# Weight copies within DRAM in small pieces, each behind a one-element read, and a plan that counts the softmax in full

## The chip, the cores and the metric

The kernel runs on one core of one Trainium2 chip. The metric is device time in microseconds (us) for one execution; lower is better. Five engines work from queues of their own: TensorE (PE, matmuls, with PEld its weight loads), VectorE (DVE), ScalarE (ACT), GpSimd (POOL) and SyncE (SP, which here issues transfers only). An engine takes its instructions strictly in order; between engines there are semaphores. A transfer is issued by SP, POOL or ACT and carried out by 16 DMA engines that they share. Unless a text says "the median", times are those of one profiled execution.

## The reference

A layer normalisation feeds two branches whose results are added to the input: a windowed attention and a ReLU network of two layers. All is in float32.

```
x: 2048 x 576;  wqkv: 576 x 1728;  wo: 576 x 576;  w1: 576 x 4608;  w2: 4608 x 576
xn  = (x - mean) / sqrt(var + 1e-5)
qkv = xn @ wqkv                      # 32 heads of 18
logits[s, w] = q[s] . k[s - 2 w] * 18**-0.5,   w = 0..7, masked where s - 2 w < 0
attn = softmax over the 8 offsets;   o[s] = sum_w attn[s, w] v[s - 2 w]
out = x + o @ wo + relu(xn @ w1) @ w2
```

## The kernel before

**Tiles and stages.** The 2048 rows are taken in two phases of 1024 (even and odd rows); a dilation of 2 stays within a phase. A phase is 8 tiles of 128 rows, in two halves. The 4608 columns of w1 go in 18 sets of 256. One pass is one set for one half, so there are 18 x 2 passes in a phase and 72 in all (`g` = 0 to 71, set `m = g // 2`). In a pass TensorE makes h transposed, 128 columns of w1 by 256 rows at a time (four such blocks a pass), and then multiplies the h of the pass before by w2 into the PSUM banks `po`. Float32 products are built of rounded high and low parts: ACT writes the high part of a block (`hhi`, with the ReLU), DVE the low part (`hlo`), and three products are summed. From the third set on, a pass computes its four blocks in seven steps (P1, P5, P6, P2, P7, P3, P4) in a Strassen manner, for which DVE forms sums of parts of w1 (`ts`) and ACT and DVE split them into `wset`.

**Attention** is done for 8 heads at a time (a unit, four in a phase). In the passes of sets 0, 3, 7 and 11 of the first phase (1, 4, 8 and 12 of the second) TensorE makes q, k and v of the unit (`qkv_tile`, into `pm`), the halo rows of k and v are shifted by transfers, and then VectorE does the attention of the unit as background work: 8 products with k and 8 sums over 18 (`pr`, `lg`), the softmax (`sm_max`, `sm_sub` with an exponential on ACT, `sm_sum`, `sm_rcp`, `sm_div`), then products with v and adds, and a transpose. The result goes through DRAM (`turned`) and is multiplied by wo some passes later. POOL sets the mask (`affine_select`, line 862) and clears two rows ahead of each unit (`memset`, lines 793 and 794).

**The order of the work.** `Order` (lines 54 to 187) decides while the program is built in which order each engine gets its instructions. TensorE's order is written out by hand: `pe` gives its next group, and before it does, `step` gives out all ACT and DVE operations that the plan's own clocks would start by then, the one with the earliest due time first. The operations of the attention (`later`) wait in a list of their own (`back`) and go in, in order, where DVE would be free. So the plan's idea of how long a DVE or ACT operation takes, for DVE `n / 960.0 + 0.062` us with `n` elements per partition (line 143), settles which instructions stand ahead of which. In `attention` the softmax is entered as `add(sm_max, n, [z])`, then `sm_sub` with a lag of 0.8, `sm_sum` with `n`, `sm_rcp` with 64 and `sm_div` with `n`, where `n` is 512 (lines 940 to 944).

**Weight copies.** Each part of the weights is first copied within DRAM into a packed tile of its own: `W1C[n]` (576 x 256) and `W2C[n]` (256 x 576) for each set, `WQC[u]` for each unit, `WOC` (lines 399 to 417). POOL issues these copies, one transfer for each. Nothing holds a copy back but what stands ahead of it in POOL's queue. SP's loads of weights into SBUF read the packed tiles and wait for the copies (`set_make`, `w2_make`, `wq_make`, `wo_make`); SP's queue is in order too. Places in the passes are given by `at(g, idx, f, ...)`: `f` is called at tick `idx` of pass `g`, a tick being one group of matmuls. The copies of set 1 stand in the prologue, after the loads of x (lines 1123 and 1124); those of a later set `m` stand in pass `2 m - 3`.

Of the kernel before, what the change touches and what calls it, by code (L numbers as in the profile page):

```python
# [16 lines left out]
P = 128  # L17
# [10 lines left out]
QP = ((0, 3, 7, 11), (1, 4, 8, 12))  # L28
# [25 lines left out]
class Order:  # L54
# [92 lines left out]
    def later(self, fn, n, after=(), lag=0.0):  # L147
        op = Op(DVE, n / 960.0 + 0.062, fn, after, FAR, lag)
        self.back.append(op)
        return op  # L150

# [39 lines left out]
def tile_body(ctx: ExitStack, tc: tile.TileContext, x, wqkv, wo, w1, w2, out):  # L191
# [211 lines left out]
    O16 = dram.tile([P, NI, DR], F32, name="o16")  # L403
    kept = {}

    def w1_keep(n):
        kept["w1", n] = o_.keep(lambda: nc.gpsimd.dma_start(W1C[n], w1[:, 2 * n * P : 2 * (n + 1) * P]), 590)

    def w2_keep(n):
        kept["w2", n] = o_.keep(lambda: nc.gpsimd.dma_start(W2C[n], w2[2 * n * P : 2 * (n + 1) * P, :]), 590)  # L410

    def wq_keep(u):
        src = wqkv.rearrange("r (s c) -> r s c", s=3)[:, :, u * UD : (u + 1) * UD]
        kept["wq", u] = o_.keep(lambda: nc.gpsimd.dma_start(WQC[u], src), 1000)

    def wo_keep():
        kept["wo"] = o_.keep(lambda: nc.gpsimd.dma_start(WOC, wo), 1300)

    SETOK = {}
    ts_free = [[]]  # L420
# [7 lines left out]
    def set_early(m):  # L428

        src = W1C[m % NP][0:256, P : 2 * P].rearrange("(k p) c -> p k c", p=P)  # L430
        TSGOT[m] = send(lambda: nc.sync.dma_start(TS[:, 1], src), 128, [kept["w1", m % NP], *ts_free[0]])

    def set_make(m, plain=False, fine=False):

# [7 lines left out]
        def rest_rows():  # L442
            for rows in slice(0, DR), slice(DR, P):
                got[RR] = send(
                    lambda rows=rows: nc.sync.dma_start(z[rows, RR].rearrange("p k c -> p (k c)"), W1C[n][KT * P : D, :]),
                    64, [kept["w1", n], *free], late,
                )

        for rows, f, s in ((0, 0, B11), (0, 1, B12), (256, 1, B22), (256, 0, B21)):
            if s == B12 and m in TSGOT:  # L450
                got[s] = TSGOT.pop(m)
                rest_rows()
                continue
            ts = s == B12 and not plain
            dst = TS[:, 1] if ts else z[:, s]
            src = W1C[n][rows : rows + 256, f * P : (f + 1) * P].rearrange("(k p) c -> p k c", p=P)
            got[s] = send(
                lambda dst=dst, src=src: nc.sync.dma_start(dst, src), 128, [kept["w1", n], *free, *(ts_free[0] if ts else [])], late
            )
            if s == B12:  # L460
                rest_rows()
# [37 lines left out]

    def w2_make(m, f):  # L500
        W2[m, f] = w = w2p.tile([P, 2, D], F32R, name="w2t")
        g = send(lambda: nc.sync.dma_start(f32(w[:, 1]), W2C[m % NP][f * P : (f + 1) * P]), 295, [kept["w2", m % NP]], 4.0)
        W2OK[m, f] = hi_lo(w[:, 0], w[:, 1], f32(w[:, 1]), D, [g], 7 + 2 * f)

    WQOK = {}
# [1 line left out]
    def wq_make(p, u, kts, raw=None):  # L507

        w = wqset(p)
        b = (p + 1) % 2  # L510
        v = wqkv.rearrange("r (s c) -> r s c", s=3)[:, :, u * UD : (u + 1) * UD] if raw is not None else WQC[u]
        for kt in kts:
            z = raw[:, kt] if raw is not None else f32(w)[:, 1, kt]
            after = [] if raw is not None else [kept["wq", u]]
# [13 lines left out]
    def wo_make(ph, u):  # L528
        WO[ph, u] = w = vp.tile([P, 2, D], F32R, name="v")
        z = f32(w)[:, 1]  # L530
        got = []
        if u < NU:
            got.append(send(lambda: nc.sync.dma_start(z, WOC[u * UD : u * UD + P, :]), 295, [kept["wo"]], 3.0))
        else:
            for b in (0, DR):
                for v in range(NU):
                    got.append(send(
                        lambda b=b, v=v: nc.sync.dma_start(z[b + 16 * v : b + 16 * v + 16], WOC[v * UD + P : (v + 1) * UD, :]),
                        37, [kept["wo"]], 3.0,
                    ))  # L540
        WOOK[ph, u] = hi_lo(w[:, 0], w[:, 1], z, D, got, 8)

# [9 lines left out]
    def h_alloc(key):  # L552
        H[key] = hp.tile([P, TBN], F32R, name="hhi"), hp.tile([P, TBN], F32R, name="hlo")

    def h_parts(key, src, after, slack, alloc=True):

        def high():
            h_alloc(key)
            copy(H[key][0], src, AF.Relu)

        def low():
            hi, lo = H[key]
            nc.vector.scalar_tensor_tensor(lo, src, 0.0, f32(hi), op0=ALU.max, op1=ALU.subtract)  # L563
# [270 lines left out]
    def attention(ph, u, halo):  # L834
# [34 lines left out]

        def sm_sub():  # L870
            nc.vector.tensor_tensor(s["lg"], s["lg"], spread(s["m"]), op=ALU.subtract)
            nc.scalar.activation(s["lg"], s["lg"], AF.Exp, scale=scale)

        def sm_sum():
# [89 lines left out]
    for m in range(2, NPH * NP):  # L964
# [12 lines left out]
    at(14, 4, w1_keep, 0)  # L977
    at(14, 5, w2_keep, 0)
    for m in range(2, NPH * NP):
        for f in range(2):  # L980
            at(2 * m - 1, 2 * f, w2_make, m, f)
# [200 lines left out]
    set_make(1, True)  # L1182
    for f in range(2):
        w2_make(1, f)
    halo(0, 0)
    classic(1, 1, 0, "bk2")
    classic(1, 1, 1, "bkA")
# [68 lines left out]
```

## Time and profile before

| what | value |
|---|---|
| median of 3 runs | 1171.18 us (1170.12 to 1175.57) |
| profiled execution, its own time | 1173.04 us |
| its span | 1171.2 us |
| TensorE busy | 1135.0 us, 97% of the span |
| VectorE busy | 819.2 us, 70% |
| ScalarE busy | 754.1 us, 64% |
| GpSimd busy | 63.4 us, 5% |
| moved by DMA | 115.6 MB, 28.9 MB of it by POOL's queue |

A row of the groups of instructions has the source line, engine and operation, the tiles written and read, a count, the busy time, the mean duration of one and the idle time of the engine ahead of them. A row of the timeline has the start and the duration in us, and in brackets how long the engine had been idle and what ended that. A row of the waits has who waited for whom, the total in us, how often and the longest. A row of the transfers has the size of one and the median time from issue to landing. A row of the windows has the stretch, its length and TensorE's busy time in it, the granted clock, the share of the DMA engines and GB/s. In the profile w1's opening loads go into a tile named `v`, and those of the opening qkv weights into `kk`.

### The profile page before, as it was taken

What the parts mean: (1) busy time and instruction counts of PE and PEld (TensorE: products, weight loads), DVE (VectorE), ACT (ScalarE), POOL (GpSimd) and SP (SyncE); (2) the same over time, 40 slices, a digit from 0 to 9 for tenths busy, and PEclk for the clock granted to TensorE, in tenths of its full rate; (3) what the DMA queues carried; (4) which work ended last, traced back from release to release, by engine and by line L of the source; (5) the groups of instructions that cost most, each with busy time, mean ns of one, the idle gap of its engine ahead of it and who ended that gap; (6) DMA issues with size and microseconds to landing.
All of it is one profiled execution on the core that took longest, in us unless ns stands there. A gap on an engine that the chain in (4) does not pass through costs nothing.

```text
span 1171.2 us, 21895 instructions
## 1 busy us (share of the span) xinstructions
PE 1135.0 (97%) x8528; PEld 1115.0 (95%) x8528; DVE 819.2 (70%) x1533; ACT 754.1 (64%) x1658; POOL 63.4 (5%) x97
## 2 busy tenths in 40 slices
PE   7999999999998999999989999999999999999998
PEld 6899999999998999999989999999999999999998
DVE  6649979952998169964783299589926995399831
ACT  5558567755766477676685577477737765576764
POOL 2200201010011001000110000000000000000000
PEclk8999999999999999999999999999999999999999
DMA  6442532762245232433262222231323212321322
GB/s 202 156 121 67 167 97 73 243 188 73 74 145 181 45 97 71 133 83 115 90 192 66 71 70 64 41 106 49 96 45 90 70 53 63 93 62 57 74 76 91
DMA packets 133544, 115.60 MB, mean 99 GB/s; under 512 B 54128, under 2 KB 112240, under 8 KB 133120
## 3 DMA queue, kind: packets, MB, share of 16 engines
q1 hardware_dynamic: 128192, 85.00, 26.1%
q0 software_dynamic: 5104, 28.90, 7.7%
q8 instruction: 67, 1.10, 0.4%
q14 instruction: 37, 0.30, 0.1%
q10 hardware_dynamic: 144, 0.29, 0.1%
HBM read 96.01 MB, written 36.50 MB: 113 GB/s over the span
## 4 chain that ended last, share of the span: by engine, by line
PE 69%; DVE 19%; DMA 5%; ACT 4%; issue 3%; POOL 0%; SPq 0%; POOLq 0%; DVEq 0%; ACTq 0%
PE po L285 29%; PE bk L285 20%; PE pm L285 15%; PE bkA L285 4%; DVE pr L886 2%; DVE hlo L563 2%; DVE wset L282 2%; DVE pr L893 2%; DVE lg L859 2%; DMA olo<-turned 2%; DVE ts L282 1%; DVE pr L856 1%; DMA wset<-w1c 1%; ACT po L279 1%; DVE sn L282 1%
## 5 line engine op out<-in xcount | busy, mean ns | idle before, releaser
L285 PE MATMUL po<-w2t,hhi 128*128 128x256 f32 (+1 forms) x2304 | 397.2, 294 | 2.4 <-ACT po L279 2.4
L285 PEld LDWEIGHTS po<-w2t,hhi 128*128 128x128 f32 x2304 | 335.9, 188 | 4.5 <-ACT po L279 3.6
L279 ACT ACTIVATE x<-po 128x576 f32<-128x576 f32 x286 | 185.6, 649 | 147.5 <-PE po L285 144.0
L285 PE MATMUL po<-w2t,hlo 128*128 128x256 f32 (+1 forms) x1152 | 244.6, 293 | 0.7 <-DVE hlo L563 0.7
L285 PE MATMUL bk<-xs,wset 128*128 128x256 f32 x1632 | 234.4, 279 | 8.5 <-DVE hlo L563 8.5
L285 PEld LDWEIGHTS bk<-xs,wset 128*128 128x128 f32 x1632 | 212.0, 189 | 12.7 <-DVE hlo L563 12.2
L285 PEld LDWEIGHTS po<-w2t,hlo 128*128 128x128 f32 x1152 | 190.7, 188 | 0.9 <-DVE hlo L563 0.9
L279 ACT ACTIVATE po<-x 128x576 f32<-128x576 f32 x286 | 186.9, 654 | 6.2
L285 PE MATMUL pm<-wset,xa 128*128 128x432 f32 x768 | 171.8, 360 | 1.1 <-DVE wset L282 0.9
L285 PEld LDWEIGHTS pm<-wset,xa 128*128 128x128 f32 x768 | 140.5, 188 | 8.5 <-DVE wset L282 1.9
L285 PE MATMUL bk<-xa,wset 128*128 128x256 f32 x924 | 132.6, 281 | 7.0 <-ACT xa L279 4.0
L285 PEld LDWEIGHTS bk<-xa,wset 128*128 128x128 f32 x924 | 120.8, 191 | 8.4 <-ACT xa L279 4.3
L282 DVE TENSOR_TENSOR sn<-bk,sn 128x256 f32<-128x256 f32 x136 | 57.3, 421 | 97.7 <-PE bk L285 55.5
L279 ACT ACTIVATE kk<-pm 128x144 f32<-128x144 f32 (+1 forms) x68 | 21.1, 310 | 121.8 <-PE pm L285 120.0
L282 DVE TENSOR_TENSOR w2t<-w2t 128x576 fp32r<-128x576 f32 (+1 forms) x72 | 53.9, 748 | 64.2 <-ACT w2t L279 63.8
L279 ACT ACTIVATE hhi<-sn 128x256 fp32r<-128x256 f32 x136 | 56.1, 413 | 46.7 <-DVE sn L282 45.5
L886 DVE TENSOR_TENSOR pr<-lg,v 128x1152 f32<-128x1152 f32 x64 | 85.1, 1352 | 0.1
L856 DVE TENSOR_TENSOR pr<-qo,kk 128x1152 f32<-128x1152 f32 x64 | 84.6, 1350 | 0.0
L859 DVE TENSOR_REDUCE lg<-pr 128x64 f32<-128x1152 f32 x64 | 84.2, 1344 | 0.0
L285 PE MATMUL bk<-xr,wset 128*128 128x256 f32 x426 | 83.7, 278 | 0.0
L282 DVE TENSOR_TENSOR wset<-wset 128x512 fp32r<-128x512 f32 (+2 forms) x120 | 71.5, 600 | 12.7 <-ACT wset L279 12.4
L279 ACT ACTIVATE wset<-wset 128x512 fp32r<-128x512 f32 (+2 forms) x120 | 65.4, 550 | 10.4 <-DMA wset<-wqc 8.3
(132 smaller groups left out, 1355.2 us busy)
## 6 DMA issues: line engine op xcount, KB each, us to landing
w2t<-w2c SPq DMA_DIRECT2D x70, 288.0 KB, 3.0
wset<-w1c SPq DMA_DIRECT2D x106, 128.0 KB, 2.4
w1c<-in_w POOLq DMA_DIRECT2D x18, 576.0 KB, 7.9
w2c<-in_w POOLq DMA_DIRECT2D x18, 576.0 KB, 8.7
wset<-wqc SPq DMA_DIRECT2D x28, 216.0 KB, 2.7
out<-x SPq DMA_DIRECT2D x16, 288.0 KB, 2.2
wset<-w1c SPq DMA_DIRECT2D x70, 64.0 KB, 2.2
ts<-w1c SPq DMA_DIRECT2D x34, 128.0 KB, 2.6
```

The lines of the kernel that those rows point to most:

```text
L279: nc.scalar.activation(o, i, func)
L282: nc.vector.tensor_tensor(o, a, b, op=op)
L285: nc.tensor.matmul(o, l, r, start=start, stop=stop, skip_group_check=True)
L563: nc.vector.scalar_tensor_tensor(lo, src, 0.0, f32(hi), op0=ALU.max, op1=ALU.subtract)
L856: nc.vector.tensor_tensor(pr[i], q, window(k, i), op=ALU.mult)
L859: nc.vector.tensor_reduce(s["lg"][:, i], pr.pop(i).rearrange(heads, d=Dh), axis=AX.X, op=ALU.add)
L886: nc.vector.tensor_tensor(pr[i].rearrange(heads, d=Dh), e, window(v, i).rearrange(heads, d=Dh), op=ALU.mult)
L893: nc.vector.tensor_tensor(o, z[:, 0:n], z[:, n : 2 * n], op=ALU.add)
```

## The change

Three things change.

1. A copy within DRAM is cut into 4 pieces (w1 and w2 of a set), 6 (a unit's qkv weights) or 8 (wo). There were 41 copies and there are 176 pieces, of 147 to 166 KB. Ahead of each piece POOL copies one element of the `hhi` that was given out last (`LATEST`) into `spare`. Every piece has a place of its own: the pieces of w1 for set `m` at ticks 0, 2, 4 and 6 of pass `2 m - 3`, those of w2 at ticks 1, 3, 5 and 7 of pass `2 m - 2`, and so on.
2. The copies of set 1 move from the prologue's loads to behind the seventh tile's transposes, and those of w1 for set 2 into the prologue behind them.
3. The plan counts `sm_max` and `sm_sum` with `2 n`, `sm_rcp` with `n - 30`, and the exponential as an ACT operation of its own with no due time; every DVE operation gets 0.068 instead of 0.062 us, every ACT operation 0.07 instead of 0.06.

TensorE's instructions stay in their order. On SP, one unit's five transfers of the turned result move behind nine others; on ACT and DVE many operations trade places.

```diff
     def act(self, fn, n, after, slack, lag=0.0):
-        op = Op(ACT, n / 1120.0 + 0.06, fn, after, self.now() + slack, lag)
+        op = Op(ACT, n / 1120.0 + 0.07, fn, after, self.now() + slack, lag)
...
     def dve(self, fn, n, after, slack, lag=0.0):
-        op = Op(DVE, n / 960.0 + 0.062, fn, after, self.now() + slack, lag)
+        op = Op(DVE, n / 960.0 + 0.068, fn, after, self.now() + slack, lag)
...
-    def w1_keep(n):
-        kept["w1", n] = o_.keep(lambda: nc.gpsimd.dma_start(W1C[n], w1[:, 2 * n * P : 2 * (n + 1) * P]), 590)
-
-    def w2_keep(n):
-        kept["w2", n] = o_.keep(lambda: nc.gpsimd.dma_start(W2C[n], w2[2 * n * P : 2 * (n + 1) * P, :]), 590)
...
+    LATEST = []
+
+    def kept_part(key, dst, src, kb):
+
+        def f():
+            nc.gpsimd.tensor_copy(spare[0:1], f32(LATEST[-1])[0:1, 0:1])
+            nc.gpsimd.dma_start(dst, src)
+
+        kept.setdefault(key, []).append(o_.keep(f, kb))
+
+    def w1_keep(n, z):
+        rows = slice(144 * z, 144 * (z + 1))
+        kept_part(("w1", n), W1C[n][rows], w1[rows, 2 * n * P : 2 * (n + 1) * P], 147)
+
+    def w2_keep(n, z):
+        kept_part(("w2", n), W2C[n][64 * z : 64 * (z + 1)], w2[2 * n * P + 64 * z : 2 * n * P + 64 * (z + 1), :], 147)
...
             h_alloc(key)
+            LATEST.append(H[key][0])
             copy(H[key][0], src, AF.Relu)
...
             nc.vector.tensor_tensor(s["lg"], s["lg"], spread(s["m"]), op=ALU.subtract)
+
+        def sm_exp():
             nc.scalar.activation(s["lg"], s["lg"], AF.Exp, scale=scale)
...
-        a = add(sm_max, n, [z])
-        a = add(sm_sub, n, [a], 0.8)
-        a = add(sm_sum, n, [a])
-        add(sm_rcp, 64)
+        a = add(sm_max, 2 * n, [z])
+        a = add(sm_sub, n, [a])
+        a = act(sm_exp, n, [a], FAR)
+        a = add(sm_sum, 2 * n, [a])
+        add(sm_rcp, n - 30)
         add(sm_div, n)
...
         if m < NP:
-            at(max(2, g - 1), 0, w1_keep, m)
-            at(max(2, g - 1), 2, w2_keep, m)
+            for z in range(4):
+                if m > 2:
+                    at(g - 1, 2 * z, w1_keep, m, z)
+                at(g, z if m == 2 else 2 * z + 1, w2_keep, m, z)
     for u in range(NU):
-        at(2 * QP[0][u] - 3 if u else 12, 4, wq_keep, u)
-    at(8, 4, wo_keep)
...
+        for z in range(6):
+            at(2 * QP[0][u] - 3 + z // 3 if u else 13 + z // 3, 4 * (z % 3) + 3, wq_keep, u, z)
+    for z in range(8):
+        at(7 + z // 4, 3 * (z % 4) + 2, wo_keep, z)
...
         x_first(i)
-    w1_keep(1)
-    w2_keep(1)
...
     turn_one(7)
+    for z in range(4):
+        w1_keep(1, z)
+    for z in range(4):
+        w2_keep(1, z)
```

More of the change, by code (lines that the diff above doesn't have):

```diff
@@ L147, in later @@
     def later(self, fn, n, after=(), lag=0.0):
-        op = Op(DVE, n / 960.0 + 0.062, fn, after, FAR, lag)
+        op = Op(DVE, n / 960.0 + 0.068, fn, after, FAR, lag)
         self.back.append(op)
@@ L404, in tile_body, with wq_keep, wo_keep @@
     kept = {}
-    def w1_keep(n):
-        kept["w1", n] = o_.keep(lambda: nc.gpsimd.dma_start(W1C[n], w1[:, 2 * n * P : 2 * (n + 1) * P]), 590)
-    def w2_keep(n):
[L410 to L417, printed above, removed]
+    LATEST = []
[9 more added lines that the diff above has]
+        kept_part(("w2", n), W2C[n][64 * z : 64 * (z + 1)], w2[2 * n * P + 64 * z : 2 * n * P + 64 * (z + 1), :], 147)
+    def wq_keep(u, z):
+        rows = slice(96 * z, 96 * (z + 1))
+        src = wqkv.rearrange("r (s c) -> r s c", s=3)[rows, :, u * UD : (u + 1) * UD]
+        kept_part(("wq", u), WQC[u][rows], src, 166)
+    def wo_keep(z):
+        rows = slice(72 * z, 72 * (z + 1))
+        kept_part(("wo",), WOC[rows], wo[rows], 166)
     SETOK = {}
@@ L445, in rest_rows @@
                     lambda rows=rows: nc.sync.dma_start(z[rows, RR].rearrange("p k c -> p (k c)"), W1C[n][KT * P : D, :]),
-                    64, [kept["w1", n], *free], late,
+                    64, [*kept["w1", n], *free], late,
                 )
@@ L457, in set_make @@
             got[s] = send(
-                lambda dst=dst, src=src: nc.sync.dma_start(dst, src), 128, [kept["w1", n], *free, *(ts_free[0] if ts else [])], late
+                lambda dst=dst, src=src: nc.sync.dma_start(dst, src), 128, [*kept["w1", n], *free, *(ts_free[0] if ts else [])], late
             )
@@ L501, in w2_make @@
         W2[m, f] = w = w2p.tile([P, 2, D], F32R, name="w2t")
-        g = send(lambda: nc.sync.dma_start(f32(w[:, 1]), W2C[m % NP][f * P : (f + 1) * P]), 295, [kept["w2", m % NP]], 4.0)
+        g = send(lambda: nc.sync.dma_start(f32(w[:, 1]), W2C[m % NP][f * P : (f + 1) * P]), 295, kept["w2", m % NP], 4.0)
         W2OK[m, f] = hi_lo(w[:, 0], w[:, 1], f32(w[:, 1]), D, [g], 7 + 2 * f)
@@ L513, in wq_make @@
             z = raw[:, kt] if raw is not None else f32(w)[:, 1, kt]
-            after = [] if raw is not None else [kept["wq", u]]
+            after = [] if raw is not None else list(kept["wq", u])
             free = slots_free(b, range(432 * kt // 256, min(7, (432 * kt + 431) // 256) + 1))
@@ L532, in wo_make @@
         if u < NU:
[L533 removed]
+            got.append(send(lambda: nc.sync.dma_start(z, WOC[u * UD : u * UD + P, :]), 295, kept["wo",], 3.0))
         else:
@@ L538, in wo_make @@
                         lambda b=b, v=v: nc.sync.dma_start(z[b + 16 * v : b + 16 * v + 16], WOC[v * UD + P : (v + 1) * UD, :]),
-                        37, [kept["wo"]], 3.0,
+                        37, kept["wo",], 3.0,
                     ))
@@ L1175, in tile_body @@
     turn_one(7)
+    for z in range(4):
+        w1_keep(1, z)
+    for z in range(4):
+        w2_keep(1, z)
     s1 = s_forms(1, 32)
@@ L1184, in tile_body @@
         w2_make(1, f)
+    for z in range(4):
+        w1_keep(2, z)
     halo(0, 0)
```

6 lines of the change are left out of this document (3 added, 3 removed).

## The prediction

> **What bounds the kernel now.** I read the page first, then TensorE's busy time in stretches, then what TensorE waited for in those stretches.
>
> ```profile
> PE 1135.0 (97%) x8528; PEld 1115.0 (95%) x8528; DVE 819.2 (70%) x1533; ACT 754.1 (64%) x1658; POOL 63.4 (5%) x97
> ```
> ```profile
> 0.00:35.00 35.00, 25.24 (x136) 0.85 0.53 169
> ...
> 200.00:540.00 340.00, 332.82 (x2533) 0.99 0.42 121
> 540.00:620.00 80.00, 72.22 (x558) 0.98 0.47 142
> 620.00:1140.00 520.00, 515.70 (x3914) 1.00 0.25 68
> ```
>
> TensorE is the bound: 1135.0 of 1171.2 us busy. Its instructions and their order stay, so the change can win only from the idle rest, some 36 us, and can lose by adding idle time. Length less busy time gives the idle time of each stretch: 9.76 us in the opening, 7.18 from 200 to 540 (the first phase's main part), 7.78 at the change of phase, 4.30 in the second phase up to 1140.
>
> Who ended TensorE's waits, in the windows 0 to 35, 200 to 540 and 620 to 1140:
>
> ```profile
> PE bk L285 <- ACT xa L279: 4.0, 1, 4.0
> ...
> PE bk L285 <- DVE hlo L563: 3.2, 6, 1.0
> PE bk L285 <- DVE sn L282: 2.8, 3, 2.3
> PE po L285 <- ACT po L279: 1.1, 2, 0.6
> ...
> PE bk L285 <- DVE hlo L563: 4.3, 8, 1.0
> ```
>
> The second phase has no copies and waits for nothing but `hlo`, 8 times for 4.3 us. The first phase's stretch has the same kind for 3.2 us and others beside it. That comparison carries much of what follows.
>
> **The change part by part.** *The opening.* The copies of set 1 leave the first 11 us. A piece of the chain, POOL's first transfers, ACT's rows and the first matmul of the network, each from its view:
>
> ```profile
> 2.78 8.12 DMA v<-in_w
> ```
> ```profile
> 1.46 0.80 POOL L407 DMA_DIRECT2D w1c<-in_w  x1
> 2.25 0.53 POOL L410 DMA_DIRECT2D w2c<-in_w  x1
> ```
> ```profile
> 7.68 0.71 ACT L279 ACTIVATE wset<-v 128x256 fp32r<-128x256 f32 x2
> 10.98 0.42 ACT L279 ACTIVATE wset<-v 128x256 fp32r<-128x256 f32 x1 [2.59 <-DMA v<-in_w]
> ...
> 13.18 3.37 PE L285 MATMUL bk<-xa,wset 128*128 128x256 f32 x12 [4.00 <-ACT xa L279]
> ```
>
> A load of w1's last rows, issued at 2.78, takes 8.12 us to land, behind 1.18 MB of copies; ACT sits idle 2.59 us for it. Without the copies ahead of it, that load lands well before ACT's two earlier roundings end at 8.39, so ACT's chain, and with it the first matmul, comes 2.59 us earlier. What is late next is ACT itself, from 6 us on without a gap. Bounds: 0 (another load is as late) and 4.0 (the whole wait). I take 2.6, since what follows to 31 us is DVE's work in order, which moves along. The moved copies go out around 51 to 62 us, where SP issues nothing; nothing for that.
>
> *The bursts.* Copies that no semaphore holds go out in one go as soon as POOL is let loose by the mask (line 862) or a memset:
>
> ```profile
> 201.22 0.68 POOL L407 DMA_DIRECT2D w1c<-in_w  x1
> ...
> 206.02 0.50 POOL L410 DMA_DIRECT2D w2c<-in_w  x1
> 206.51 0.93 POOL L793 MEMSET kk<- 1x1008 f32 x1
> 246.15 0.93 POOL L794 MEMSET v<- 1x1008 f32 x1 [38.71 <-ACT bkA L279]
> ```
>
> SP's loads issued from 175 to 199 and from 201 to 220 (size, median us to landing):
>
> ```profile
> wset<-w1c SPq DMA_DIRECT2D x3, 128.0 KB, 2.2
> ```
> ```profile
> wset<-w1c SPq DMA_DIRECT2D x3, 128.0 KB, 9.9
> ts<-w1c SPq DMA_DIRECT2D x1, 128.0 KB, 14.5
> ```
>
> Loads of one size take 2.2 us without and 9.9 to 14.5 with a burst beside them. Its sums are then late on DVE, and what stands behind them in DVE's order too. Price: the second phase idles 4.30 us in four units' attention; three lie between 200 and 540, so 3/4 of it, 3.2, is there without copies. The rest of 7.18, 4.0 us, I put down to the bursts. In the new kernel every piece waits for an h that is just being made, so a pass carries 4 to 7 pieces of 147 to 166 KB and no burst forms. Bounds: 0 (those waits come from DVE's order alone) to 5.1 (all of it but the `hlo` waits, with the 1.1 of `po`). I take 4.0, since `sn` 2.8 and `po` 1.1, which the second phase doesn't have, add up to just that.
>
> *The plan of the softmax.* Groups by line with shapes kept apart, and one low part with the matmul that waited for it:
>
> ```profile
> L875 DVE TENSOR_REDUCE r<-lg 128x64 f32<-128x512 f32 x8 | 9.2, 1154 | 1.8 <-ACT lg L872 1.8
> L868 DVE TENSOR_REDUCE m<-lg 128x64 f32<-128x512 f32 x8 | 9.2, 1150 | 7.5 <-POOL lg L862 7.5
> L878 DVE RECIPROCAL r<-r 128x64 f32<-128x64 f32 x8 | 4.4, 545 | 0.1
> ```
> ```profile
> 1075.77 0.42 DVE L563 SCALAR_TENSOR_TENSOR hlo<-bk,hhi 128x256 fp32r<-128x256 f32 x1
> ```
> ```profile
> 1076.24 0.97 PE L285 MATMUL bk<-xs,wset 128*128 128x256 f32 x6 [0.67 <-DVE hlo L563]
> ```
>
> The plan before gives max and sum 512/960 + 0.062 = 0.595 us each; they take 1.15. It gives the reciprocal 64/960 + 0.062 = 0.129; it takes 0.545. So each unit has 0.555 + 0.559 + 0.416 = 1.53 us of DVE work that the plan doesn't know, 12.2 us in eight units, in stretches that the background fills. DVE falls behind its plan by that, and the next `hlo` is late: TensorE waits 3.2 + 4.3 = 7.5 us for `hlo` in the two stretches. The new plan gives 1024/960 + 0.068 = 1.135 and 482/960 + 0.068 = 0.570, within 0.025 of the measured, and puts other operations between the subtraction and the sum while ACT does the exponential. No DVE work is removed; urgent operations only stand further ahead. Bounds: 0 to 7.5 won, or a loss if the new order opens waits of its own. I take three quarters, 5.6: nearest the upper end, since the missing 1.53 us is of the size of a unit's wait, and short of it, since other things can make an `hlo` late. The waits at the change of phase (7.78 us idle) lie where the softmax isn't; nothing for them.
>
> *What is added on POOL.* 176 one-element reads and 176 issues. Rows for bounds:
>
> ```profile
> 1.25 0.10 POOL L230 MEMSET mhalf<- 128x1 f32 x1
> 5.86 0.24 POOL L320 TENSOR_SCALAR nm<-mv 128x1 f32<-128x1 f32 x1 [3.08 <-DVE mv L317]
> ```
> ```profile
> L407 POOL DMA_DIRECT2D w1c<-in_w x18 | 11.9, 663 | 0.1
> L321 POOL TENSOR_TENSOR rstd<-mv,mhalf 128x1 f32<-128x1 f32 x16 | 9.5, 595 | 130.6 <-DVE mv L318 130.5
> L862 POOL TENSOR_SCALAR_AFFINE_SELECT lg<-lg 1x512 f32<-1x512 f32 x8 | 9.1, 1138 | 707.2 <-DVE lg L859 707.2
> ```
>
> A read costs 0.10 to 0.60 us, I take 0.24 of the nearest form; an issue at most the 0.66 of a whole copy. That is at most 176 x (0.24 + 0.66) = 158 us of POOL in some 495 us, on an engine that is 5% busy: no bound. POOL's reads can hold DVE up, though. One sum that began during the mask took 1.19 us, where its kind takes 0.44:
>
> ```profile
> 200.15 1.10 POOL L862 TENSOR_SCALAR_AFFINE_SELECT lg<-lg 1x512 f32<-1x512 f32 x1 [72.11 <-DVE lg L859]
> ```
> ```profile
> 200.26 1.19 DVE L282 TENSOR_TENSOR ts<-ts,wset 128x256 f32<-128x256 f32 x1
> ```
> ```profile
> L282 DVE TENSOR_TENSOR ts<-ts,wset 128x256 f32<-128x256 f32 x34 | 15.0, 441 | 23.6 <-DMA wset<-w1c 23.6
> ```
>
> That is 0.75 us of 9.1 us of mask; I take a tenth of POOL's reading time as lost to DVE. 176 x 0.24 = 42 us gives some 4 us of DVE; half the DVE operations lie in the first phase, and 0.006 us more for each of some 770 gives the plan 4.6 us of room. So little reaches TensorE: 1 us. Bounds: 0 and 42.
>
> *What waits for the pieces.* SP's load of a set waits for its pieces, and all of SP's queue behind it. One block's high part in two passes, and POOL's loads of x:
>
> ```profile
> 172.67 0.37 ACT L279 ACTIVATE hhi<-bkA 128x256 fp32r<-128x256 f32 x1
> ...
> 184.74 0.37 ACT L279 ACTIVATE hhi<-bkA 128x256 fp32r<-128x256 f32 x1
> ```
>
> ```profile
> x<-in_x POOLq DMA_DIRECT2D x8, 288.0 KB, 3.5
> ```
>
> A pass lasts 12.1 us and has 15 ticks. The last piece of w1 goes out at tick 6, about 5 us into the pass before the load's place; a POOL load of 288 KB lands in a median of 3.5 us, so about 3 us are left. If they are gone, DVE's sums wait, then the `hlo` behind them. The read also ties ACT to POOL: five buffers of `hhi` at four a pass last 15 us, so ACT waits only when POOL is over 15 us late; between the units' memsets it has nothing to be late by. For both together 1 us; bounds 0 and 2.2 (a lone load) for each of 16 sets, 35.
>
> Sum: 2.6 + 4.0 + 5.6 - 1 - 1 = 10.2 us. Against the profiled execution's own 1173.04 that is 1162.8. The median of the runs stands 1.86 below that execution, so for the median 1161.0.
>
> **The rivals.** *Little is won:* the bursts only hid what DVE's order does anyway, and the new order opens as many waits as it closes. Then the opening's 2.6 and half of the softmax's, 2.8, less 2, are left: 3.4 us, 1167.8. For it: even the first phase idles only 2%, and about 250 rows of DVE's order change place. Against it: the waits that only the first phase has. This holds too if the pieces still go out in heaps because their reads find an old h, as the first 12 do.
>
> *Pieces too late (slower):* place, SP's queue in the first phase; mechanism, a piece lands after its load's turn, SP stands, `ts` and then `hlo` are late. It decides from 0.64 us a set on (10.2 over 16) and makes the kernel slower by 2.2 a set: 35 less the other gains of 12.2 less 1, +24, so about 1195. Against it: 3 us of room a pass, and the set loaded in one pass is used a pass later.
>
> *POOL holds VectorE up (slower):* mechanism, each read stops a DVE operation for all its 0.24 us, where DVE is already full; 42 us on the path less 12.2 won, plus 1: +31, about 1202. It decides from 12.2/176 = 0.07 us a read on. For it: the row of 1.19; against it: one stretch of that size beside 8 masks. [...]
>
> **How the numbers follow.** The forecast (10 us faster) has 0.74, little won 0.13, late pieces 0.08, held-up DVE 0.05. A difference of 0.5%, 5.9 us, is about what a measurement of this kernel can tell from none. So faster 0.74, same 0.13, slower 0.13. Range: all terms at their better ends give 2.6 + 5.1 + 7.5 = 15, 1156; with the opening at 4.0 1154.6, so 1154 below; above, 1172 takes in the little-won case with an added us or four and leaves out most of the slower ones. The forecast's own range is 1155 to 1165.
>
> **What the profile after would show.** First matmul of `bk` near 10.6 us instead of 13.18. No stretch in which SP's w1 loads take over 5 us. TensorE's idle time from 620 to 1140 down from 4.3 to about 1, and from 200 to 540 from 7.2 to about 2. POOL's reads near 0.24 us, and no DVE sum stretched beyond that. The prediction is wrong if SP's waits on `w1c` or ACT's waits on POOL appear with microseconds each, or if `hlo` waits stay in the second phase, where only the plan has changed.

## The result, and the profile after

| | before | changed |
|---|---|---|
| median | 1173.16 us (1170.12 to 1175.57, 4 runs) | 1155.41 us (1153.78 to 1159.75, 4 runs) |
| ratio to before | | 0.9856, 95% interval 0.9815 to 0.9896 |
| profiled execution, its own time | 1173.04 us | 1153.78 us |
| its span | 1171.2 us | 1152.0 us |
| TensorE busy | 1135.0 us | 1126.6 us |
| TensorE idle (span less busy) | 36.2 us | 25.4 us |

The kernel became faster by 1.4%, where 10.2 us (0.9%) were forecast. The predicted 1161.0 us lies 5.6 us above the measured median; that median, 1155.41, lies just inside the forecast's own range of 1155 to 1165. Idle time fell by 10.8 us, close to the forecast sum; busy time fell by 8.4 us more, although TensorE does the same work. That part was not foreseen.

The profile after, first its engines, then TensorE in the stretches used before (start, end, length, busy time, granted clock, share of the DMA engines, GB/s):

```profile
PE 1126.6 (98%) x8528; PEld 1111.0 (96%) x8528; DVE 822.0 (71%) x1533; ACT 754.0 (65%) x1658; POOL 201.3 (17%) x408
```
```profile
0.00:35.00 35.00, 27.83 (x160) 0.90 0.45 135
35.00:200.00 165.00, 160.49 (x1181) 1.00 0.44 123
200.00:540.00 340.00, 338.17 (x2606) 1.00 0.45 123
540.00:620.00 80.00, 73.17 (x572) 0.98 0.47 144
620.00:1140.00 520.00, 518.73 (x3956) 1.00 0.26 69
```

The opening idles 7.17 instead of 9.76 us, the stretch from 200 to 540 1.83 instead of 7.18, the second phase 1.27 instead of 4.30. One stretch is worse: 35 to 200, 4.51 instead of 2.13, by this row of before from the same view:

```profile
35.00:200.00 165.00, 162.87 (x1194) 1.00 0.39 115
```

The waits of TensorE after, in the windows 35 to 200 (two rows), 200 to 540 (two) and 620 to 1140 (one):

```profile
PE bk L285 <- DVE sn L282: 2.4, 2, 1.3
...
PE bk L285 <- DVE hlo L577: 0.7, 1, 0.7
...
PE po L285 <- ACT po L279: 0.9, 1, 0.9
PE bk L285 <- DVE hlo L577: 0.9, 2, 0.7
...
PE po L285 <- ACT ohi L279: 1.3, 1, 1.3
```

The 4.3 us of `hlo` waits in the second phase are gone; what is left there is one wait at the kernel's end. The first matmul of `bk` in the changed kernel's timeline, SP's loads of w1 issued from 201 to 220 us, and POOL's reads in the groups by line with the pieces of w1 among the page's transfers:

```profile
10.84 1.01 PE L285 MATMUL bk<-xa,wset 128*128 128x256 f32 x3 [1.62 <-ACT xa L279]
```
```profile
wset<-w1c SPq DMA_DIRECT2D x3, 128.0 KB, 3.0
...
ts<-w1c SPq DMA_DIRECT2D x1, 128.0 KB, 3.2
```
```profile
L411 POOL COPY spare<-hhi 1x1 f32<-1x1 f32 x176 | 78.1, 444 | 291.4 <-ACT hhi L279 291.4
```
```profile
w1c<-in_w POOLq DMA_DIRECT2D x72, 144.0 KB, 2.7
```

The first matmul stands at 10.84 instead of 13.18 us; loads that took 9.9 and 14.5 us now take 3.0 and 3.2. Elsewhere, from 163 to 166 us, four loads of w1 take 5.4 to 5.8 us, where the forecast had none over 5. A read takes 0.444 us in the mean, not the 0.24 of the forecast.

### The profile page after: what moved, and what is told of

It reads as the page before. It is cut to its first block, busy times and chain, and to the rows that moved or that the text cites. A ratio compares the mean times of both kernels' runs of the same rounds, so it can differ in the third digit from the quotient of the medians.

```text
span 1152.0 us, 22365 instructions
## 1 busy us (share of the span) xinstructions
PE 1126.6 (98%) x8528; PEld 1111.0 (96%) x8528; DVE 822.0 (71%) x1533; ACT 754.0 (65%) x1658; POOL 201.3 (17%) x408
## 4 chain that ended last, share of the span: by engine, by line
PE 87%; DVE 4%; DMA 3%; ACT 3%; issue 1%; SPq 1%; POOL 0%; ACTq 0%; DVEq 0%; POOLq 0%
PE po L285 40%; PE bk L285 27%; PE pm L285 15%; PE bkA L285 6%; DMA x<-in_x 1%; DVE wset L282 1%; ACT po L279 1%; ACT x L279 1%; ACT wset L279 1%; DMA turned<-pr 1%; DMA wset<-wqc 0%; DVE hlo L577 0%; DMA qo<-in_w 0%; SPq L551 0%; DVE ts L282 0%
## 5 line engine op out<-in xcount | busy, mean ns | idle before, releaser
L285 PE MATMUL bk<-xs,wset 128*128 128x256 f32 x1632 | 231.9, 278 | 2.1 <-DVE hlo L577 2.0
L411 POOL COPY spare<-hhi 1x1 f32<-1x1 f32 x176 | 78.1, 444 | 291.4 <-ACT hhi L279 291.4
```

Source lines behind the costliest of these rows:

```text
L285: nc.tensor.matmul(o, l, r, start=start, stop=stop, skip_group_check=True)
L411: nc.gpsimd.tensor_copy(spare[0:1], f32(LATEST[-1])[0:1, 0:1])
```

## The experiments

Each run is given as its ratio to the kernel before, measured on the same chip, with its 95% interval; 0.001 is 1.2 us.

### The three parts, one at a time

The plan alone: the kernel before with both of the plan's changes and nothing else.

```diff
# before
-        op = Op(ACT, n / 1120.0 + 0.06, fn, after, self.now() + slack, lag)
+        op = Op(ACT, n / 1120.0 + 0.07, fn, after, self.now() + slack, lag)
...                                  # dve and later alike, 0.062 to 0.068
-        a = add(sm_max, n, [z])
+        a = add(sm_max, 2 * n, [z])
...                                  # sm_sub to sm_rcp as in the change
```

> The kernel before with the new plan of VectorE alone (costs, softmax counted in full, exponential as its own operation); copies as before. Three separate gains (theory): the waits for hlo in the second phase go (4.3 us idle to under 1), those of the first phase from 200 to 540 partly; the first matmul of bk stays near 13.2 us and SP's w1 loads still take about 10 us in the bursts. Time 6 to 9 us under before. Rival (all comes from the copies): second phase unchanged, time within 2 us of before.

Measured: 0.9908 (0.9890 to 0.9925), 1161.48 us. The plan is worth 10.8 us by itself, about twice the term of the forecast. TensorE's waits for `hlo` fall to 0.4 us from 200 to 540 and to nothing in the second phase up to 1140; from 200 to 540 it still waits 3.2 us for `sn` and 3.1 us for ACT to empty `po`, and idles 6.87 us there instead of 7.18.

The copies alone: the changed kernel with the old costs and the old softmax entries.

```diff
# changed kernel
-        op = Op(ACT, n / 1120.0 + 0.07, fn, after, self.now() + slack, lag)
+        op = Op(ACT, n / 1120.0 + 0.06, fn, after, self.now() + slack, lag)
...                                  # dve and later alike, 0.068 to 0.062
-        a = add(sm_max, 2 * n, [z])
+        a = add(sm_max, n, [z])
...                                  # sm_sub to sm_rcp as before
```

> The changed kernel with the old plan of VectorE and ScalarE; pieces, reads and places as changed. Theory: first matmul of bk near 10.8 us, no SP w1 load over 6 us, no half-clock window near 378 us, but 4 to 5 us of hlo waits again in the second phase. Time 8 to 11 us under before. Rival (the plan does it all but the opening): 3 us under before, with the waits of 200 to 540 as before.

Measured: 0.9924 (0.9902 to 0.9947), 1162.95 us. TensorE idles 3.9 us from 200 to 540 and still 3.7 us in the second phase, 3.6 of it for `hlo` in 7 waits: there only the plan helps.

The opening alone: the two copies of set 1 moved, nothing else.

```diff
# before
-    w1_keep(1)
-    w2_keep(1)
...
     turn_one(7)
+    w1_keep(1)
+    w2_keep(1)
```

> The kernel before with only the two copies of set 1 moved behind the seventh tile's transposes; nothing else changes, and the order on PE, DVE, ACT and SP is that of before. Theory: first matmul of bk near 10.8 us; the half-clock window after 12.9 us is 3.4 instead of 6.8 us long; 3 to 4 us under before, all of it within the first 50 us. Rival (other loads are as late): no more than 1 us.

Measured: 0.9985 (0.9969 to 1.0001), 1171.0 us, so 1.8 us, just short of telling it from nothing. The first `bk` matmul starts at 10.66, 2.5 us earlier.

By these three the opening is worth about 1.8, the other copies about 7.2 (0.9985 less 0.9924), the plan 10.8: 19.8 us in sum, where the changed kernel won 16.9. The intervals are too wide to tell these 3 us from nothing, but the traces show a loss of that size; it is found further down.

### The plan: counts and costs

The softmax's counts alone, with the costs of before:

```diff
# before
-        a = add(sm_max, n, [z])
-        a = add(sm_sub, n, [a], 0.8)
-        a = add(sm_sum, n, [a])
-        add(sm_rcp, 64)
+        a = add(sm_max, 2 * n, [z])
+        a = add(sm_sub, n, [a])
+        a = act(sm_exp, n, [a], FAR)
+        a = add(sm_sum, 2 * n, [a])
+        add(sm_rcp, n - 30)
```

> The kernel before with only the softmax counted in full (2 n, n - 30, exponential as its own operation); the costs of single operations on VectorE and ScalarE as before, copies as before. Theory (the 1.53 us a unit that the plan lacked make the hlo late): the second phase's hlo waits fall from 4.3 us to under 1.5, 4 to 7 us under before. Rival (the 0.006 and 0.01 us on every operation do it): the second phase keeps 3 us or more and the time is within 2 us of before.

Measured: 1.0012 (0.9997 to 1.0027): nothing won. Then the costs alone:

```diff
# before
-        op = Op(ACT, n / 1120.0 + 0.06, fn, after, self.now() + slack, lag)
+        op = Op(ACT, n / 1120.0 + 0.07, fn, after, self.now() + slack, lag)
...
-        op = Op(DVE, n / 960.0 + 0.062, fn, after, self.now() + slack, lag)
+        op = Op(DVE, n / 960.0 + 0.068, fn, after, self.now() + slack, lag)
```

> The kernel before with nothing changed but the plan's cost of an operation: 0.068 instead of 0.062 us for VectorE, 0.07 instead of 0.06 for ScalarE. The softmax stays uncounted, the copies whole and where they were. The run with the softmax's counts alone won nothing (ratio 1.0012), that with counts and costs won 10.8 us (0.9908). Theory now: the costs carry the gain, since 1533 operations of VectorE at 0.006 us give the plan 9.2 us more of VectorE, near the 12.2 us that the softmax lacks, and spread over all passes instead of over eight units: about 1163 beside 1173, ratio 0.991, second phase's idle time (620 to 1140) under 2 us. Rival: only both together win, since the counts make the units late and the costs the passes: ratio 0.997 to 1.0, second phase's idle time still over 3 us.

Measured: 0.9973 (0.9959 to 0.9987), 3 us. TensorE in the window 200 to 540 of the three runs, in the order counts, costs, both:

```profile
200.00:540.00 340.00, 326.52 (x2479) 0.99 0.39 112
```
```profile
200.00:540.00 340.00, 333.48 (x2541) 0.99 0.42 122
```
```profile
200.00:540.00 340.00, 333.13 (x2536) 0.99 0.42 122
```

And from 700 to 1100, which lies inside the second phase in every run, first in the kernel before, then in the same order:

```profile
700.00:1100.00 400.00, 395.70 (x3003) 1.00 0.25 68
```
```profile
700.00:1100.00 400.00, 399.90 (x3051) 1.00 0.25 68
```
```profile
700.00:1100.00 400.00, 396.77 (x3004) 1.00 0.25 68
```
```profile
700.00:1100.00 400.00, 400.00 (x3060) 1.00 0.26 70
```

In this stretch the idle time of 4.30 us falls to 0.10 by the counts, to 3.23 by the costs and to nothing by both. So there the counts alone do what the prediction said, nearly in full, and more than the idle time is won: at the pace of 3060 matmuls in 400 us, the 48 more that TensorE makes with the counts are some 6 us of work, the 57 more with both some 7. In the first phase the counts lose it again: 13.48 us idle instead of 7.18. The largest new wait there, followed back in the run with the counts alone (a wait of TensorE, then DVE, ACT and POOL in the timeline):

```profile
PE pm L285 <- ACT qo L279: 3.9, 1, 3.9
```
```profile
253.07 2.62 DVE L888 TENSOR_TENSOR pr<-lg,v 128x1152 f32<-128x1152 f32 x2
```
```profile
255.72 0.29 ACT L279 ACTIVATE v<-pm 128x144 f32<-128x144 f32 x1 [4.60 <-DVE pr L888]
```
```profile
255.88 0.93 POOL L794 MEMSET v<- 1x1008 f32 x1 [36.13 <-issue]
```

The tile `v` of a unit can be written again only when the last product with `v` of the unit before has been made. With the counts alone that product ends at 255.7, some 10 us later than in the kernel before (245.9); ACT's copy of the next unit's `v` and POOL's memset come right behind it, and TensorE, whose `pm` bank ACT has not emptied, waits 3.9 us. With both changes it ends at about 245.3 and the wait is not there. Shown is the place and the wait; why the finer costs bring that unit in time again was not followed through the planner.

### The copies: reads, size, place and the planner's order

The changed kernel without the reads:

```diff
# changed kernel
-            nc.gpsimd.tensor_copy(spare[0:1], f32(LATEST[-1])[0:1, 0:1])
             nc.gpsimd.dma_start(dst, src)
```

> The changed kernel without the one-element reads; pieces, their order in POOL's queue and the orders on PE, DVE, ACT and SP as in the changed kernel. Theory (the reads pace the copies): pieces go out in heaps behind the mask and the memsets as before, though at most 8 are under way at a time; SP's w1 loads beside a heap take 5 to 10 us, the waits of sn and po near 215 to 230 and 370 to 380 us come back, 4 to 6 us slower than the changed kernel. Rival (small pieces and eight at a time are enough): loads stay under 5 us and the time is within 2 us of the changed kernel.

Measured: 0.9818 (0.9797 to 0.9840), 1151.94 us. Without the reads it is, if anything, faster; the two intervals overlap. Pieces do go out in heaps, and eight loads of w1, three of them issued from 210 to 212 us, take 5.4 to 6.8 us beside them. TensorE idles 1.99 us from 200 to 540, as with the reads.

The same under the old plan, the copies alone and no reads:

```diff
# the copies alone
-            nc.gpsimd.tensor_copy(spare[0:1], f32(LATEST[-1])[0:1, 0:1])
             nc.gpsimd.dma_start(dst, src)
```

> The kernel before with the copies in pieces at their new places, the old plan, and no one-element reads, so that pieces go out as soon as GpSimd has its turn. The same with the reads gave ratio 0.9924 and an idle time of TensorE of 3.9 us from 200 to 540. Theory of the prediction (bursts): without the reads heaps form again, loads of a set take 5 to 14 us beside them, and the stretch from 200 to 540 idles some 7 us as before; what is left is the opening: ratio 0.997 to 0.999. Rival, from the run without reads under the new plan: heaps cost next to nothing, and the gain comes from where the copies stand: ratio 0.992, idle time of that stretch 4 us.

Measured: 0.9926 (0.9910 to 0.9942), the 0.9924 of the run with reads. The reads do nothing there either.

But cutting and moving the copies also changes what the planner believes, and with it the order of DVE, ACT and SP. So the last run keeps exactly that order and puts the whole copies of the kernel before back to their old places, with set 1 out of the opening:

```diff
# the copies alone, without reads
-    def kept_part(key, dst, src, kb):    # a piece is counted and not sent:
+    def kept_part(key):
+        kept.setdefault(key, []).append(o_.keep(lambda: None, 166 if key[0][1] in "qo" else 147))
...
+    def real(key):                       # sends one whole copy
...
+            at(max(2, g - 1), 0, real, ("w1", m))
+            at(max(2, g - 1), 2, real, ("w2", m))
...
+        at(2 * QP[0][u] - 3 if u else 12, 4, real, ("wq", u))
+    at(8, 4, real, ("wo",))
...
```

> Only what the planner believes of the copies is changed, and the opening. The old plan's costs; the planner is told of 176 pieces at their new places, so that VectorE, ScalarE and SyncE get exactly the order of the run in pieces without reads (ratio 0.9926); the transfers themselves are 41 whole copies at the places of the kernel before (set 1 moved out of the opening, as in the run of the opening alone, 0.9985), with nothing to hold them. Theory of the prediction (bursts): heaps of whole copies slow the loads as before, and the first phase idles for it: 0.997 to 0.999, idle time of TensorE from 200 to 540 about 7 us. Rival: the transfers matter little and the order that the planner makes of them is what won: 0.992 to 0.994, idle time of that stretch about 5 us, with loads of w1 of 8 us and more still there.

Measured: 1.0005 (0.9992 to 1.0019). The order alone wins nothing, and with DVE, ACT and SP in the same order the transfers are worth 0.0079, some 9 us. TensorE in 200 to 540, first with the pieces, then with the whole copies:

```profile
200.00:540.00 340.00, 334.82 (x2567) 1.00 0.42 118
```
```profile
200.00:540.00 340.00, 327.29 (x2488) 0.99 0.40 112
```

The 7.5 us between them come to about the 7.4 us between the two spans (1163.7 and 1171.1). Most of it is one place. In the run with whole copies: TensorE's longest wait, ACT at 226.85, and a load of wo issued at 212.7; last, ACT at the same operation in the run with pieces:

```profile
PE po L285 <- ACT po L279: 7.0, 2, 6.1
```
```profile
226.85 0.68 ACT L279 ACTIVATE v<-v 128x576 fp32r<-128x576 f32 x1 [4.60 <-DMA v<-woc]
```
```profile
v<-woc SPq DMA_DIRECT2D x1, 288.0 KB, 14.1
```
```profile
222.23 0.67 ACT L279 ACTIVATE v<-v 128x576 fp32r<-128x576 f32 x1
```

Five whole copies are issued at 210.8 to 214 behind the mask; the load of wo beside them takes 14.1 us (6.3 with the pieces), ACT stands 4.6 us for it, and what ACT does next, emptying `po`, is what TensorE waits 6.1 us for.

The kernel before has the same thing at another place. POOL's copies (first and last of six), ACT and TensorE behind them, and TensorE from 370 to 384; then the changed kernel at the same work:

```profile
361.86 0.65 POOL L407 DMA_DIRECT2D w1c<-in_w  x1
...
364.75 0.50 POOL L410 DMA_DIRECT2D w2c<-in_w  x1
```
```profile
374.57 0.56 ACT L279 ACTIVATE wset<-wset 128x432 fp32r<-128x432 f32 x1 [3.43 <-DMA wset<-wqc]
```
```profile
376.53 0.96 PE L285 MATMUL bk<-xa,wset 128*128 128x256 f32 x6 [2.26 <-DVE sn L282]
```
```profile
370.00:384.00 14.00, 11.23 (x75) 0.88 0.68 189
```
```profile
364.33 0.55 ACT L279 ACTIVATE wset<-wset 128x432 fp32r<-128x432 f32 x1
```
```profile
358.00:372.00 14.00, 14.00 (x118) 1.00 0.49 135
```

Six copies let loose by the memset of `v` drive the loads of the qkv weights, issued from 365.3 on, to 8 and 9 us; ACT waits 3.43 us, DVE's sums for `sn` come late behind that, TensorE waits 2.26 us and then 0.51, and runs at a granted clock of 0.50 from 378.1 to 381.6 (0.88 in the mean of the row). In the changed kernel the same stretch has no gap.

Size was tried with the reads in place: whole copies, each behind one read, where its first piece stood.

```diff
# changed kernel
     def w1_keep(n, z):
-        rows = slice(144 * z, 144 * (z + 1))
-        kept_part(("w1", n), W1C[n][rows], w1[rows, 2 * n * P : 2 * (n + 1) * P], 147)
+        if z:
+            return
+        rows = slice(0, D)
+        kept_part(("w1", n), W1C[n][rows], w1[rows, 2 * n * P : 2 * (n + 1) * P], 590)
...                                  # w2, wq and wo alike
```

> The changed kernel with whole copies again (one for each part of the weights, 576 to 1296 KB), each behind one read, in the place of its first piece. Theory (what counts is that copies are spread over the passes): one copy a pass, SP's w1 loads up to 4 or 5 us, time within 3 us of the changed kernel. Rival (the size counts: a whole copy beside SP's loads is a burst of its own): loads of 6 us and more, waits of sn or ts, 5 us or more slower than the changed kernel.

Measured: 0.9856 (0.9834 to 0.9878), the ratio of the changed kernel to four places. That looks as if the size did not matter, but the equality is a coincidence of two differences. The planner counts a whole copy otherwise than a piece, and VectorE, ScalarE and SP get another order than in the changed kernel. TensorE in this run from 35 to 200 and from 200 to 540, and its longest wait there:

```profile
35.00:200.00 165.00, 162.65 (x1205) 1.00 0.44 130
200.00:540.00 340.00, 335.16 (x2561) 0.99 0.42 120
```
```profile
PE pm L285 <- ACT qo L279: 3.7, 1, 3.7
```

The first stretch idles 2.35 us, where the changed kernel idles 4.51 (the next section says why); the second 4.84 instead of 1.83, mostly by a wait of the kind that the softmax's counts alone opened: ACT's copy of `v` stands behind a late product with `v`. VectorE waits for a load only once in this run from 120 to 250 us, for 0.65 us, so that late product points at the order and not at slow loads; what the size alone costs stays open. What the run does show is that whole copies, kept apart by reads, slow the loads far less: its slowest load of w1 takes 6.6 us, where the kernel before has up to 14.5. So the slow loads go in two ways, by pieces without reads and by reads without pieces. Whole copies at the new places without reads were not tried, so what the places alone do stays open.

Four reads instead of one ahead of each piece, to see what reading costs:

```diff
# changed kernel
-            nc.gpsimd.tensor_copy(spare[0:1], f32(LATEST[-1])[0:1, 0:1])
+            for _ in range(4):
+                nc.gpsimd.tensor_copy(spare[0:1], f32(LATEST[-1])[0:1, 0:1])
```

> The changed kernel with four reads ahead of each piece instead of one. If POOL's reads hold VectorE up for their length (0.18 us each, 704 reads), VectorE's sums are stretched and the kernel is 10 us or more slower. Theory from the trace of the changed kernel, where reads were stretched to 6.9 us beside VectorE's products and none of VectorE's operations beside a read by more than 0.1 us: VectorE stays as it is, POOL is busy some 200 us more, the time within 3 us of the changed kernel unless pieces come late.

Measured: 0.9906 (0.9875 to 0.9937), some 6 us slower than the changed kernel by the ratios, whose intervals overlap, and 5.5 by the profiled spans (1157.5 and 1152.0). Around 480 to 500 us, POOL (two rows) and ACT (two rows) in the timeline, then TensorE's wait:

```profile
478.32 6.05 POOL L412 COPY spare<-hhi 1x1 f32<-1x1 f32 x4
...
484.82 5.64 POOL L412 COPY spare<-hhi 1x1 f32<-1x1 f32 x4
```
```profile
491.91 0.39 ACT L279 ACTIVATE hhi<-bkA 128x256 fp32r<-128x256 f32 x1 [2.15 <-POOL spare L412]
...
497.35 0.68 ACT L279 ACTIVATE w2t<-w2t 128x576 fp32r<-128x576 f32 x1 [3.64 <-DMA w2t<-w2c]
```
```profile
PE po L285 <- ACT po L279: 2.0, 1, 2.0
```

Here both mechanisms of the prediction appear that cost nothing with one read: ACT waits for POOL to let go of a buffer of `hhi`, and a load of w2 comes late because its pieces do (SP waits for pieces of w2 94.9 us in 25 waits, in the changed kernel 35.9 us in 12). VectorE is not held up: the 64 products with `v` take 1353 ns each, in the kernel before 1352.

### The transfers of the turned result

In the changed kernel SP issues the turned result of the first unit behind nine other transfers. One line sends them first again, by having the planner give out all background work before the next set's loads:

```diff
# changed kernel
+            at(g + 1, 4, lambda: o_.force(list(o_.back)))
             at(g + 1, 4, set_make, p + 1, False, True)
```

> The changed kernel, but the background list of DVE is given out in full just before a unit's following set is prepared, so that SP sends the turned result of the first unit ahead of the second unit's halo, as in before. Theory: the 5.61 us that DVE waits for the transfer of pr at 162 to 168 us in the changed kernel are due to that place in SP's queue and go; TensorE's waits at 172 to 178 (3.1 us idle) go with them: 3 to 4 us under the changed kernel. Rival (the DMA engines are full there with the pieces of wo and w2): the transfers are as late as before and nothing is won.

Measured: 0.9812 (0.9790 to 0.9834), 1150.31 us, the fastest of all. By the medians that is 5 us under the changed kernel, with intervals that overlap; by the profiled spans (1152.0 and 1148.8) 3.2. The turned transfers in SP's timeline and DVE's wait for them, in the changed kernel; then SP with the line added; then DVE in the run without reads:

```profile
158.91 4.13 SPq L923 DMA_DIRECT2D turned<-pr  x4
```
```profile
168.28 1.36 DVE L870 TENSOR_TENSOR pr<-qo,kk 128x1152 f32<-128x1152 f32 x1 [5.61 <-DMA turned<-pr]
```
```profile
152.06 2.25 SPq L923 DMA_DIRECT2D turned<-pr  x4
```
```profile
164.95 1.36 DVE L869 TENSOR_TENSOR pr<-qo,kk 128x1152 f32<-128x1152 f32 x1 [2.31 <-DMA turned<-pr]
```

The turned result leaves from `pr`, and DVE's next product writes `pr`. In the changed kernel DVE stands 5.61 us for it; what is late behind it are `sn` and `hlo`, for which TensorE waits three times between 172 and 179 us, 1.07 + 1.31 + 0.68 = 3.1 us. With the line added DVE does not wait for these transfers, and TensorE waits 0.85 and 0.20 us there, for others. That is the loss that the sum of the parts lacked: with the plan alone DVE waits 2.1 us there, and with the copies alone TensorE idles only 1.9 us from 35 to 200. In the run without reads the wait is 2.31 us and TensorE does not notice: no pieces ran beside those transfers, whose median landing time was 3.7 us against 4.7. This would explain why that run came out faster: not the reads as such but where they put the pieces. Both together:

```diff
# changed kernel
+            at(g + 1, 4, lambda: o_.force(list(o_.back)))
...
-            nc.gpsimd.tensor_copy(spare[0:1], f32(LATEST[-1])[0:1, 0:1])
```

> The kernel after with the turned transfers of a unit ahead of the next set's loads again, and without the one-element reads: no piece is held by anything but its place in the queue of GpSimd. Theory: the run without reads gained its 4 us on the kernel after only because no pieces ran beside the turned transfers at 159 to 168 us; with those transfers early there is nothing left to gain, so the time is that of the kernel with the order alone, ratio 0.981 (about 1150 beside 1173), within 2 us. Rival: the reads cost of themselves, by holding ScalarE's next high part or VectorE up: then both gains add, 0.978 (about 1147). Other rival: the reads matter with this order and the heaps cost: 0.984 or more.

Measured: 0.9827 (0.9810 to 0.9845), 1153.51 us, not to be told from the order alone. With the turned transfers early, the reads win or lose nothing that can be measured.

## Why the prediction was right, and where it was wrong

That the time lies in the range is in part luck. The three gains were priced too low in sum (12.2 us, where the parts measured 19.8) and a loss was left out, and the two offset each other: with that loss undone by one line the median is 1150.31 us, outside the range.

**The opening (2.6 us): right.** The load came early and ACT's chain with it, 2.34 us; the opening idles 2.6 us less. As a whole it measured 1.8 us alone.

**The bursts (4.0 us): the mechanism right, the carrier wrong and the size too small.** Heaps of copies do slow SP's loads until TensorE waits, and the transfers, at the same order of DVE, ACT and SP, are worth some 9 us. But the loads of w1 at 201 to 220, which the prediction showed, are not where it costs most; that is the loads of the qkv weights behind the memset of `v` at 361. And "no burst forms" because each piece waits for an h is not needed: small pieces without reads form heaps that do next to no harm (from 200 to 540 TensorE idles 1.99 us instead of 1.83, under the old plan 5.2 instead of 3.9).

**The plan of the softmax (5.6 us): the mechanism right in the second phase, the price wrong.** There the counts alone take the `hlo` waits away, 4.2 of 4.3 us, as forecast. By themselves they lose it again in the first phase: the loss that the bounds named ("if the new order opens waits of its own") happened in the run with the counts alone. The forecast took the 0.006 us an operation for room that pays for POOL's reads; the costs are worth 3 us alone, and only both together win 10.8, about twice the term.

**POOL's reads (-1 us) and waiting for pieces (-1 us): nothing measurable.** No operation of VectorE took over 0.1 us more than the median of its kind, except beside masks as before (four for `olo` took 0.68 to 0.84 us, their median is 0.42); 36 us more of reading than forecast (78.1 against 42) went by beside it. SP did wait for pieces in the changed kernel, 79.6 us in 7 waits at one line of the set's loads, which the prediction had named as a sign of its failure. That sign was badly chosen: the loads are issued long before they are used, and TensorE saw none of it.

**SP's moved transfers (no term): wrong.** The turned result moved behind nine transfers, which the sum put at nothing without a reason. It cost 3.1 us of waits, and 3 to 5 us by the run that undoes it (whose line also shifts some of DVE's background work).

**Left out altogether: TensorE's busy time.** That "the change can win only from the idle rest" was wrong. Of the 19.2 us between the spans 8.4 are busy time: the waits cost more than their idle time here. In part the clock is lower behind a wait (below). The stretches at a granted clock of 0.50, without the kernel's end, make 17.1 us before (12.9 to 19.7, 30.0 to 33.4, 378.1 to 381.6 and 617.1 to 620.5) and 10.2 after (10.4 to 13.8, 27.5 to 30.9 and 583.8 to 587.2); at half the clock the 6.8 us between them come to 3.4 of the 8.4. In part they cost more at a clock of 1.00 too: from 700 to 1100 us 4.3 us of idle time went and some 7 us of work were won, so some 3 us of busy time lie there, in 8 waits. The remaining 2 us were not traced, nor what stretches the work around a wait.

**The rivals.** That little would be won falls with the ratio. That pieces come too late, and that ACT is tied to POOL, needs four reads a piece, and the two then cost about 6 us together. That VectorE is held up did not happen at all: it was POOL's reads that took longer (below).

## What to carry to other kernels

Price a slow load by the wait that it ends in, not by its own length: beside the loads of 9.2 to 14.5 us TensorE waited 1.7 us in all, behind those of 8 to 9 us 2.8 us and ran at a clock of 0.50 for 3.4 us after it. When a change moves an order that a planner makes, ask for every queue what now stands ahead of what; the transfers that were moved without a price cost 3 to 5 of the some 20 us that the parts won. Two small corrections to a plan's costs need not add up: 0 and 3 us apart were 11 together. And equal times need not mean equal kernels: before a run is said to change nothing, compare its waits too.

## What the runs showed of the hardware

*Some waits of TensorE were followed by a slow stretch.* Granted clock around waits, in the run with whole copies and the planner's order (a wait of 6.1 us), the run with the softmax's counts (3.9 us) and the changed kernel (1.07, 1.31 and 0.68 us):

```profile
220.00:240.00 20.00, 13.67 (x94) 0.83 0.41 124
```
```profile
254.00:262.00 8.00, 5.75 (x19) 0.57 0.48 159
```
```profile
165.00:181.00 16.00, 12.94 (x101) 1.00 0.60 178
```

In windows of 1 us the clock of the kernel before and of the changed kernel reads 1.00 or 0.50, and something between only where it changes. Behind the wait of 2.26 us in the kernel before it reads 0.57, 0.50, 0.50 and 0.72 from 378 to 382, which is 3.4 us at 0.50. If the two runs with longer waits have no other values either, 0.17 of 20 us is 6.8 us at 0.50 and 0.43 of 8 us is 6.9. By that estimate such a wait lost another 1.7 to 3.4 us of work, and the waits of up to 1.31 us in this stretch of the changed kernel lost none. Not every wait did: in the kernel before, at the change of phase, waits of 2.05 and 1.29 us leave the clock at 1.00:

```profile
592.00:606.00 14.00, 10.67 (x87) 1.00 0.57 172
```

So 2.26 us without work were followed by a stretch at 0.50, and 2.05 us were not; what decides it is not shown.

*A one-element read on POOL took longer beside VectorE's work, and did not hold VectorE up.* In the changed kernel a single read takes 0.177 us in the median. The longest, 6.94 us from 467.75 on, lies beside two products with `v` and eight adds of VectorE; these two products take 1.36 us each, where the kernel before has 1.352 in the mean. In the run with four reads, four took 6.05 and 5.64 us in all, and the products with `v` 1.353 in the mean. The forecast had feared the other direction. What makes a read take so long was not shown; no run varied it.
